# Top-k attention and an ELU layer on one core: scores at the head of a step, the last keys' chunk turned with the first half, values a step later

## Chip, cores and metric

One core of one Trainium2 chip runs the whole program as one launch. The metric is device time in microseconds (us); lower is better. The engines are called PE (TensorE matmuls; PEld are its weight loads), DVE (VectorE), ACT (ScalarE), POOL (GpSimd) and SP (SyncE, here a queue of DMA issues).

## What is computed

Eight batches of eight heads, 576 rows, head size 64. Of each row of scores only the 32 largest count; then a softmax, and the product with the values. The heads side by side are the rows of a layer with 2048 hidden columns and ELU between its two products.

```python
scores = scale * np.matmul(q, k.transpose(0, 1, 3, 2))
kth = np.partition(scores, -32, axis=-1)[..., -32:-31]
scores = np.where(scores >= kth, scores, -1e9)
attn = softmax(scores)                 # with 1e-9 added to the sum
x = np.matmul(attn, v)                 # (B,H,S,D) -> (B*S, H*D) = 4608 x 512
h = x @ w_in                           # 512 -> 2048
out = np.where(h > 0, h, np.exp(np.minimum(h, 0)) - 1) @ w_out   # 2048 -> 512
```

## The kernel before

**Steps.** A batch's 576 queries are four tiles of 128 (`qt` 0 to 3) and one of 64 (`qt` 4); a step is one such tile with a pair of heads (of the small tile, four heads). There are 144 steps. Each passes through four stages in successive steps of one loop (L809): in step n the scores of step n + 2 are computed (`ahead`), DVE selects the 32 largest of step n (`cur`), ACT and POOL mask and normalise step n - 1 (`prev`), and PE turns the weights of step n - 2 (`done`).

**Stages.** `scores` (L326) runs four matmuls, two per head, into two wide PSUM tiles (`wide[0]`, `wide[1]`, one per head, printed as scps), which ACT copies to SBUF (L343). `select` is a generator with four passes of DVE's MAX8 and MATCH_REPLACE8 (L355 to L369). `spread` (L376) takes the gap between threshold and maximum on POOL, `mask` (L396, L397) makes the exponentials on ACT, once per head, and `normalise` (L407 to L414) divides on POOL. `turn` (L418) transposes the weights on PE and copies them on ACT (L434) into a tile `et`: four chunks of keys of the first head (`main`), the chunk that holds the last 64 keys of both heads (`rest`), and four chunks of the second head (`other`). `main` and `other` use two PSUM tiles in turn (eps); `rest` uses free columns of `wide[1]`, the tile of the second head's scores. When the last step of a group (one tile or a pair) has been turned, the group is appended to `closing`, and `attend` (L443) multiplies it with the values (avps) and copies the result to `xT` (L486).

**The layer.** When a block's `xT` is complete (a block has one or two slots of 128 rows; the first five and the last have one, fifteen have two), `ffn_pieces` appends its work to a list: sixteen `hidden` pieces (four accumulated matmuls each, L534), whose results ACT reads in groups (L544 to L553), and then the second product: for one slot four `project` pieces (L562), for two slots seven `product` pieces (L624) of a scheme with seven block products, for which POOL combines the operands (L580) and SP streams kept differences of weights (`tw`, L666). A piece has a nominal cost in us: hidden 1.1 or 1.85, project and product 3.55.

**The order.** Every engine executes its instructions in the order in which the loop writes them. `feed` is called four times a step (the quarters q1 to q4) and takes as many pieces as a plan allows: each block has a due time in steps (`ready`, L728) and the cost of all blocks ahead of it (L729 to L733), and the rate is the smallest of what is left to each due time, so that the pieces last until the next block is ready (L772). So PE gets, in step n: q1, scores, attention, q2, main, q3, rest, other, q4. ACT's copies and masks stand between in the same order. `load_v` and `load_halves` are put on SP at fixed steps ahead of a batch; a value tile is one of five buffers and is loaded again when its last `attend` is done.

Of the kernel before, what the change touches and what calls it, by code (L numbers as in the profile page):

```python
# [80 lines left out]
def kernel(  # L81
# [119 lines left out]
    def hook():  # L201

        if decode:
            decode.pop(0)()
# [121 lines left out]
    def scores(u):  # L326

        u.sc = scpool.tile([P, 2, S], FP32, tag="sc", name="sc")
        q0 = (QUERIES if u.t.b == 0 else S) + u.t.qt * P
        for half in range(2):  # L330
            for h, i, rows in u.heads:
                kq = kqT[u.t.b, h // 2]
                part = slice(i * D, (i + 1) * D)
                k0 = (KEYS if i == 0 and u.t.b == 0 else 0) + half * HS
                nc.tensor.matmul(  # L335
                    wide[i][rows, half, 0:HS],
                    kq[part, q0 : q0 + u.t.ql],
                    kq[part, k0 : k0 + HS],
                    start=True,
                    stop=True,  # L340
                )
        for i in range(2):
            nc.scalar.activation(  # L343
                u.sc[:, i, :].rearrange("p (a s) -> p a s", a=2),
                wide[i][:, :, 0:HS], AF.Copy, scale=scale,
            )

    def select(u, more=False):

        u.first = small.tile([P, 2, 8], FP32, tag="m1", name="m1")  # L350
        u.last = small.tile([P, 2, 8], FP32, tag="m4", name="m4")
        cur = [u.sc[:, i, :] for i in range(2)]
        found = [u.first[:, i, :] for i in range(2)]
        for i in range(2):
            nc.vector.max(found[i], cur[i])  # L355
        if more:
            hook()
        yield
        wk = [wkpool.tile([P, S], FP32, tag=f"wk{i}", name="wk")[:] for i in range(2)]
        for r in range(TOP_K // 8 - 1):  # L360
            for i in range(2):
                nc.vector.match_replace(wk[i], found[i], cur[i], TAKEN)  # L362
            cur = wk
            for i in range(2):
                if r < TOP_K // 8 - 2:
                    found[i] = small.tile([P, 8], FP32, tag=f"m{i}", name="m")[:]
                else:
                    found[i] = u.last[:, i, :]
                nc.vector.max(found[i], cur[i])  # L369
            hook()  # L370
            yield
# [46 lines left out]
    def turn(u, chunks):  # L418

        if u.turned:  # L420
            return
        g = u.group
        if g.et is None:
            g.et = etpool.tile([P, 2 * J + 1, len(g.tiles), P], FP32, tag="et", name="et")
        if chunks.stop - chunks.start == 1:
            ps = wide[1][:, 1, HS : HS + P]
        else:
            ps = ps_t.tile([P, JP], FP32, tag="t", name="eps")
        sc = u.sc[:, :, :].rearrange("p i s -> p (i s)")
        n = chunks.stop - chunks.start  # L430
        for c in range(n):
            c0 = (chunks.start + c) * P
            nc.tensor.transpose(ps[:, c * P : (c + 1) * P], sc[:, c0 : c0 + P], ident[:])  # L433
        nc.scalar.copy(  # L434
            g.et[:, chunks, u.at, :],
            ps[:, 0 : n * P].rearrange("p (c q) -> p c q", c=n),
        )
        if chunks.stop == 2 * J + 1:
            u.turned = True
            if u.at == len(g.tiles) - 1:  # L440
                closing.append(g)

    def attend(g):  # L443
        t = g.tiles[0]
        ps = ps_t.tile([P, JP], FP32, tag="t", name="avps")
        n = P if t.rem else sum(x.ql for x in g.tiles)
        for k in range(2 if t.rem else 1):
            hp = 2 * g.hp + k if t.rem else g.hp
            vt = vT[t.b, hp]
            for c in range(J + 1):  # L450
                for i in range(2):
                    chunk = J if c == J else i * (J + 1) + c
                    w = g.et[:, chunk, :, :].rearrange("p a q -> p (a q)")
                    cols = slice(0, n)
                    if t.rem:
                        c0 = R * (k if i == 0 else 1 - k)
                        w = w[:, c0 : c0 + R]
                        cols = slice(k * R, (k + 1) * R)
                    nc.tensor.matmul(  # L459
                        ps[i * D : (i + 1) * D, cols],  # L460
                        vt[:, 2 * J + i if c == J else i * J + c, :],
                        w,
                        start=(c == 0),
                        stop=(c == J),
                    )
        if t.rem:
            finish(t.block, 2, slice(2 * g.hp, 2 * g.hp + 2), t.cols,
                   ps[:, 0:n].rearrange("p (a q) -> p a q", a=2))
            return
        c0 = 0  # L470
        tiles = list(g.tiles)
        while tiles:
            blk, lo, parts = tiles[0].block, tiles[0].cols.start, 0
            while tiles and tiles[0].block is blk:
                parts += 1
                hi = tiles.pop(0).cols.stop
            finish(blk, parts, g.hp, slice(lo, hi), ps[:, c0 : c0 + hi - lo])
            c0 += hi - lo

    def finish(blk, parts, at, cols, src):  # L480
        if blk.xT is None:
            if blk.slots == 1:
                blk.xT = xpool.tile([P, NC, P], FP32, tag="xT", name="xT")
            else:
                blk.xT = late["x"].tile([P, NC, T], FP32, tag="xT", name="xT")
        nc.scalar.copy(blk.xT[:, at, cols], src)  # L486
        blk.left -= parts
        if blk.left == 0:
            ffn.extend(ffn_pieces(blk))

    gates = []
    place = [0]
# [195 lines left out]
    blocks, tight = [], 2 * NHP  # L688
# [10 lines left out]
    while ends:  # L699
        n = 1 if len(blocks) <= J else 2  # L700
# [5 lines left out]
    for b in range(B):  # L706
        first[b] = len(steps)
        tiles = []
        for qt in range(J + 1):
            r0 = b * S + (JP if qt == J else qt if b == 0 else qt * P)  # L710
            if qt == J:
                (blk, slot), c0, n = slots[b | 1, J], (b % 2) * R, R
                rows = slice(r0, r0 + R)
            else:
                (blk, slot), c0, n = slots[b, qt], 0, P
                rows = slice(r0, r0 + J * (P - 1) + 1, J) if b == 0 else slice(r0, r0 + P)
            c0 += slot * P
            t = Tile(b, qt, rows, blk, slice(c0, c0 + n))
            blk.left += NHP
            blk.tiles[slot].append(t)  # L720
            tiles.append(t)
        for qts in orders[b]:
            for hp in range(NHP // 2 if qts == (J,) else NHP):
                group = Group([tiles[qt] for qt in qts], hp)
                steps += [Step(tiles[qt], hp, group, i) for i, qt in enumerate(qts)]
            for qt in qts:
                n = len(steps)
                tiles[qt].block.ready = n + 2.0 if n <= tight else n + 2.5  # L728
    NS = len(steps)  # L729
    total = 0.0  # L730
    for blk in sorted(blocks, key=lambda x: x.ready):
# [72 lines left out]
    def step(n):  # L804
        return steps[n] if 0 <= n < NS else None

    closing = []
    main, rest, other = slice(0, J), slice(J, J + 1), slice(J + 1, 2 * J + 1)
    for n in range(NS + 3):  # L809
        for fn, args in todo.pop(n, []):  # L810
            fn(*args)
        ahead, cur, prev, done = step(n + 2), step(n), step(n - 1), step(n - 2)
        passes = select(cur, n < tight) if cur else iter(range(4))
        if prev and n > tight:
            spread(prev)
        next(passes)
        feed(n, 0.25)
        if ahead and n > 1:
            scores(ahead)
        while closing:  # L820
            attend(closing.pop(0))
        if prev:
            mask(prev, 0, n <= tight)
        if n > 1:
            turn_qk()
        next(passes)
        feed(n, 0.25)
        if done:
            turn(done, main)
        if prev:  # L830
            mask(prev, 1, n <= tight)
        next(passes)
        feed(n, 0.25)
        if done:
            turn(done, rest)
            turn(done, other)
        next(passes)
        if prev:
            normalise(prev)
        if spare and n >= first[1] - 2:  # L840
            difference(*spare.pop(0))
        feed(n, 0.25)
        turn_qk(True)
        if n < 2:
            scores(ahead)
# [36 lines left out]
```

## Time and profile before

| | |
|---|---|
| three runs | 1586.64, 1590.04, 1593.43 us; median 1590.04 |
| the profiled execution | 1590.94 us, its span 1588.4 us |
| mean granted TensorE clock | 0.988 of full speed |
| DMA | 123.47 MB, 78 GB/s |
| MAX8 over 576 columns, one | 748 ns |
| exponential with its sum over 576 columns, one | 776 ns, and 187 ns to read the sum |
| copy of 128 x 512 turned weights, one | 581 ns |
| scaling of 128 x 576 weights on POOL, one | 755 ns |

The profile comes from one execution. In its rows, "x4" is a count, and in rows in order of time the first two numbers are the start and the length in us of a run of like instructions; "[1.25 <-ACT et L434]" says that the engine was idle 1.25 us ahead of it, until ACT's operation of line 434 on the tile et was done. A matmul that the program writes once appears as two records (and two weight loads), the transposes as one.

### The profile page before, as it was taken

How to read it: one execution, taken by the hardware profiler on the slowest of the kernel's cores; microseconds unless marked ns; L12 is line 12 of the kernel's file. 1: busy time of each engine (PE TensorE's matmuls, PEld its weight loads, DVE VectorE, ACT ScalarE, POOL GpSimd, SP SyncE). 2: the span in 40 equal slices, each digit the busy share in tenths (PEclk: the TensorE clock that was granted, in tenths of full speed). 3: DMA queues.
4: the chain of work that ended last, by engine and by line, in shares of the span. 5: the costliest groups of instructions: out<-in, count | busy, mean ns of one | idle time of the engine just before them, and what ended most of it. 6: DMA issues, size and time to landing. Idle time of an engine off the chain costs nothing.

```text
span 1588.4 us, 28211 instructions
## 1 busy us (share of the span) xinstructions
PE 1516.6 (95%) x9492; PEld 1182.4 (74%) x9492; DVE 1451.2 (91%) x2976; ACT 1200.0 (76%) x2460; POOL 904.0 (57%) x1551
## 2 busy tenths in 40 slices
PE   4679999999999999999999999999999999999999
PEld 2467767767778778877887778777787777877786
DVE  6899999999999899999999699999999969999700
ACT  6897777878786868686968687868777777878652
POOL 4983455556555565646565656565655565656550
PEclk9889999999999999999999999999999999999999
DMA  8522201233405140424122323224130513030311
GB/s 242 192 80 37 38 30 56 56 70 79 120 1 150 31 135 17 132 33 127 39 91 60 97 61 88 71 65 108 50 94 27 138 42 116 19 110 1 119 54 34
DMA packets 224911, 123.47 MB, mean 78 GB/s; under 512 B 182272, under 2 KB 183296, under 8 KB 224768
## 3 DMA queue, kind: packets, MB, share of 16 engines
q1 hardware_dynamic: 223568, 121.38, 28.2%
q8 instruction: 75, 1.23, 0.3%
q14 instruction: 68, 0.56, 0.1%
q10 hardware_dynamic: 1200, 0.30, 0.1%
HBM read 108.00 MB, written 13.63 MB: 77 GB/s over the span
## 4 chain that ended last, share of the span: by engine, by line
PE 72%; ACT 12%; DVE 9%; POOL 3%; issue 3%; SPq 1%; DMA 1%; DVEq 0%; ACTq 0%; POOLq 0%
PE hps L534 24%; PE ops L624 20%; PE avps L459 10%; PE scps L335 9%; PE eps L433 6%; DVE wk L362 4%; DVE m L369 3%; PE ops L562 3%; ACT sc L397 2%; ACT sc L396 2%; ACT sc L343 2%; DVE m L355 1%; ACT et L434 1%; ACT n L553 1%; ACT n L544 1%
## 5 line engine op out<-in xcount | busy, mean ns | idle before, releaser
L369 DVE MAX8 m<-wk 128x8 f32<-128x576 f32 x864 | 610.1, 748 | 2.2 <-POOL den L376 2.2
L534 PE MATMUL hps<-xT,w_in 128*128 128x256 f32 (+1 forms) x2688 | 548.6, 353 | 0.4 <-ACT gT L547 0.4
L534 PEld LDWEIGHTS hps<-xT,w_in 128*128 128x128 f32 x2688 | 440.6, 192 | 59.7 <-issue 18.8
L362 DVE MATCH_REPLACE8 wk<-m,wk 128x576 f32<-128x576 f32 x576 | 423.7, 744 | 0.0
L407 POOL TENSOR_SCALAR dene<-den 128x2 f32<-128x2 f32 x144 | 32.8, 228 | 466.0 <-ACT sc L397 464.6
L397 ACT ACTIVATE sc<-sc,den 128x576 f32<-128x576 f32 x288 | 223.4, 776 | 55.6 <-POOL den L376 40.8
L335 PE MATMUL scps<-kqT 64*128 64x288 f32 (+1 forms) x1280 | 215.0, 445 | 52.4 <-ACT et L434 38.4
L343 ACT ACTIVATE sc<-scps 128x576 f32<-128x576 f32 x288 | 170.7, 644 | 82.9 <-PE scps L335 82.9
L396 ACT ACTIVATE sc<-sc,m 128x576 f32<-128x576 f32 x288 | 223.8, 777 | 4.8 <-DVE m L369 4.8
L624 PE MATMUL ops<-tw,gT 128*128 128x256 f32 x960 | 220.0, 382 | 2.7 <-POOL gT L580 1.3
L414 POOL TENSOR_SCALAR sc<-sc,rec 128x576 f32<-128x576 f32 x288 | 214.2, 755 | 14.9
L355 DVE MAX8 m<-sc 128x8 f32<-128x576 f32 x288 | 202.1, 744 | 11.9 <-ACT sc L343 11.9
L362 DVE MATCH_REPLACE8 wk<-m,sc 128x576 f32<-128x576 f32 x288 | 211.8, 744 | 0.0
L335 PEld LDWEIGHTS scps<-kqT 64*128 64x128 f32 (+1 forms) x1280 | 113.6, 182 | 131.4 <-ACT et L434 53.5
L624 PEld LDWEIGHTS ops<-tw,gT 128*128 128x128 f32 x960 | 177.7, 190 | 33.4 <-issue 7.3
L504 POOL TENSOR_TENSOR gT<-n,gT 128x512 f32<-128x512 f32 x136 | 173.7, 1279 | 28.9 <-ACT n L553 27.7
L459 PE MATMUL avps<-et,vT 128*64 128x256 f32 (+2 forms) x2320 | 187.5, 312 | 0.0
L459 PEld LDWEIGHTS avps<-et,vT 128*64 128x64 f32 x2320 | 127.8, 142 | 68.0 <-issue 28.5
L433 PE MATMUL eps<-ident,sc 128*128 128x128 f32 x1152 | 175.2, 277 | 0.0
L434 ACT COPY et<-eps 128x512 f32<-128x512 f32 x288 | 167.4, 581 | 9.8 <-PE eps L433 8.2
L624 PE MATMUL ops<-w_out,gT 128*128 128x256 f32 x720 | 164.2, 381 | 0.0
L433 PEld LDWEIGHTS eps<-ident,sc 128*128 128x128 f32 x1152 | 138.3, 143 | 30.8 <-issue 12.9
(56 smaller groups left out, 1536.7 us busy)
## 6 DMA issues: line engine op xcount, KB each, us to landing
tw<-kept SPq DMA_DIRECT2D x240, 256.0 KB, 3.0
raw<-in_moe_w_in_dram SPq DMA_DIRECT2D x16, 512.0 KB, 4.9
vT<-in_v_dram SPq DMA_DIRECT2D x64, 128.0 KB, 2.5
raw<-in_moe_w_out_dram SPq DMA_DIRECT2D x16, 512.0 KB, 4.0
out_dram<-osb SPq DMA_DIRECT2D x32, 256.0 KB, 3.7
kin<-in_k_dram SPq DMA_DIRECT2D x112, 72.0 KB, 2.7
qin<-in_q_dram SPq DMA_DIRECT2D x112, 72.0 KB, 2.6
kept<-tw SPq DMA_DIRECT2D x16, 256.0 KB, 2.1
```

What stands on the lines that cost most here:

```text
L335: nc.tensor.matmul(wide[i][rows, half, 0:HS], kq[part, q0 : q0 + u.t.ql], kq[part, k0 : k0 + HS], start=True, stop=True,)
L343: nc.scalar.activation(u.sc[:, i, :].rearrange("p (a s) -> p a s", a=2), wide[i][:, :, 0:HS], AF.Copy, scale=scale,)
L355: nc.vector.max(found[i], cur[i])
L362: nc.vector.match_replace(wk[i], found[i], cur[i], TAKEN)
L369: nc.vector.max(found[i], cur[i])
L396: nc.scalar.activation(sc, sc, AF.Prelu, scale=-1.0, bias=low, alpha=1.0 / STEEP)
L397: nc.scalar.activation(sc, sc, AF.Exp, scale=-STEEP, bias=gap, accum_out=u.den[:, i : i + 1])
L414: nc.gpsimd.tensor_scalar(u.sc[:, i, :], u.sc[:, i, :], rec[:, i : i + 1], 1.0, ALU.mult, ALU.mult)
L433: nc.tensor.transpose(ps[:, c * P : (c + 1) * P], sc[:, c0 : c0 + P], ident[:])
L459: nc.tensor.matmul(ps[i * D : (i + 1) * D, cols], vt[:, 2 * J + i if c == J else i * J + c, :], w, start=(c == 0), stop=(c == J),)
L534: nc.tensor.matmul(blk.h[:, f % bank, :], w_in[:, i, f * P : (f + 1) * P], blk.xT[:, i, 0:n_tok], start=(i == 0), stop=(i == NC - 1),)
L624: nc.tensor.matmul(sums, x[:, f, :], w, start=opens and f == 0, stop=f == NG - 1, skip_group_check=not opens,)
```

## The change

The scores of step n + 2 move to the head of step n, ahead of the first quarter's pieces (and ahead of `spread`). From step 12 on (`settled`) until the last step, a closed group is attended at the head of a step, right behind the scores, and only if it was closed more than one step ago; `closing` therefore holds the step in which the group was closed. Before step 12 and after the last selection the attention stays behind q1. `turn(done, rest)` moves from the third quarter to the second, right behind `turn(done, main)` and ahead of the second mask. The due times of all blocks that are ready after step 8 grow from n + 2.5 to n + 3.25.

So PE's order in a step becomes: scores, attention, q1, q2, main, rest, q3, other, q4.

```diff
         if chunks.stop == 2 * J + 1:
             u.turned = True
             if u.at == len(g.tiles) - 1:
-                closing.append(g)
+                closing.append((place[0] // 4, g))
...
-                tiles[qt].block.ready = n + 2.0 if n <= tight else n + 2.5
+                tiles[qt].block.ready = n + 2.0 if n <= tight else n + 3.25
...
-    closing = []
+    closing, settled = [], tight + 4
...
         passes = select(cur, n < tight) if cur else iter(range(4))
+        if ahead and n > 1:
+            scores(ahead)
+        steady = settled <= n < NS
+        while steady and closing and closing[0][0] < n - 1:
+            attend(closing.pop(0)[1])
         if prev and n > tight:
             spread(prev)
         next(passes)
         feed(n, 0.25)
-        if ahead and n > 1:
-            scores(ahead)
-        while closing:
-            attend(closing.pop(0))
+        while closing and not steady:
+            attend(closing.pop(0)[1])
         if prev:
             mask(prev, 0, n <= tight)
...
         if done:
             turn(done, main)
+            turn(done, rest)
         if prev:
             mask(prev, 1, n <= tight)
         next(passes)
         feed(n, 0.25)
         if done:
-            turn(done, rest)
             turn(done, other)
```

## The prediction

> **What bounds the kernel now.** I read the page first: busy shares, then the span in 40 slices.
>
> ```profile
> span 1588.4 us, 28211 instructions
> PE 1516.6 (95%) x9492; PEld 1182.4 (74%) x9492; DVE 1451.2 (91%) x2976; ACT 1200.0 (76%) x2460; POOL 904.0 (57%) x1551
> PE   4679999999999999999999999999999999999999
> DVE  6899999999999899999999699999999969999700
> ```
>
> PE and DVE are both full after the third slice. Which of them leads shows in the waits of the whole span, longest in total first (who <- whom: us, times, longest):
>
> ```profile
> ACT sc L343 <- PE scps L335: 82.9, 88, 4.0
> DVE gT L506 <- ACT n L549: 70.7, 4, 62.1
> DVE kqT L289 <- PE scps L335: 33.0, 3, 16.1
> ```
>
> DVE waits for PE, three times up to 16 us, and ends its selection 62 us before its last additions. PE is the late engine, so the time is PE's work plus PE's lost time, and the change leaves the work as it is: the same matmuls, in another order. The question is what PE loses today. Two stretches answer: from 115 us, when the FFN has begun to fill PE, to 455, and from there to the end (columns: us, busy of PE, PEld, DVE, ACT, POOL, clock, DMA).
>
> ```profile
> 115.00:455.00 340.00, 332.60 (x2206) 243.70 (x2204) 340.00 (x700) 261.02 (x534) 180.59 (x341) 0.99 0.23 57
> 455.00:1588.00 1133.00, 1115.17 (x6906) 887.82 (x6906) 1012.54 (x2084) 844.94 (x1739) 637.77 (x1085) 1.00 0.28 74
> ```
>
> PE idles 7.4 us in the first and 17.8 us in the second. The waits of PE (first two rows, 455 to the end) and of its weight loads (third row, same stretch; fourth row, 115 to 455) name the cause:
>
> ```profile
> PE scps L335 <- ACT et L434: 10.9, 12, 1.3
> PE scps L433 <- ACT sc L343: 2.3, 3, 0.8
> PEld scps L335 <- ACT et L434: 19.4, 17, 1.8
> PEld scps L335 <- ACT et L434: 9.0, 8, 2.4
> ```
>
> The scores wait for a copy of turned weights. The matmul row understates it, because a matmul record runs on after PE could have taken the next; the load row (19.4 us) is nearer. One such event, in order of time (ACT's and PE's rows):
>
> ```profile
> 450.84 0.56 ACT L434 COPY et<-eps 128x512 f32<-128x512 f32 x1
> 450.96 0.27 PE L433 MATMUL scps<-ident,sc 128*128 128x128 f32 x1
> 451.07 0.60 PE L433 MATMUL eps<-ident,sc 128*128 128x128 f32 x4
> 451.30 0.77 ACT L396 ACTIVATE sc<-sc,m 128x576 f32<-128x576 f32 x1
> 451.50 1.89 PE L534 MATMUL hps<-xT,w_in 128*128 128x256 f32 x8
> 452.88 0.58 ACT L544 ACTIVATE n<-hps 128x512 f32<-128x512 f32 x1
> 453.33 0.75 PE L335 MATMUL scps<-kqT 64*128 64x288 f32 x2
> 455.03 0.25 ACT L434 COPY et<-scps 128x128 f32<-128x128 f32 x1
> 455.33 1.24 PE L335 MATMUL scps<-kqT 64*128 64x288 f32 x6 [1.25 <-ACT et L434]
> 456.50 2.38 PE L459 MATMUL avps<-et,vT 128*64 128x256 f32 x20
> ```
>
> The last keys' chunk (`rest`, L835) is turned by PE at 450.96 into the bank of the second head's scores. Its copy stands on ACT behind the second mask (451.30 to 452.88, 1.6 us) and a pair of hidden pieces (452.88 to 455.03, 2.15 us). The scores begin at 453.33, stop after the first head's half, and end at 456.50: 3.17 us. Undisturbed they take 1.17:
>
> ```profile
> 445.79 1.24 PE L335 MATMUL scps<-kqT 64*128 64x288 f32 x8
> 446.96 1.99 PE L534 MATMUL hps<-xT,w_in 128*128 128x256 f32 x8
> ```
>
> So this event costs 2.0 us where the matmul row shows 1.25.
>
> **The change, part by part.** The sum is made against the profiled execution, 1590.9 us (span 1588.4, 2.5 around it); it lies 0.9 over the median of 1590.04.
>
> *Rest turned with main.* Removes nothing; the one transpose and the copy (0.14 us to the next operation on ACT) move ahead of the second mask and the third quarter's pieces. In the event above the copy would have started at 451.30 instead of 455.03, 3.7 us earlier and 2 us before the scores want the bank. Where a finished pair of hidden pieces now stands ahead of the main copy (q2 in the built order of the changed kernel), it comes 2.15 us later, at 453.5, and still ends 0.4 us too late; I count some eight of the fifteen two-slot blocks with such a step ahead of the scores, and three with scores right after the turning. I leave 11 x 0.5 = 5 us standing of the 19.4 after 455: **-14 us** (bounds: 0, if ACT's backlog only moves; -24, if all go and each costs 0.3 us more than its load row, as 2.0 against at most 1.8 above suggests).
>
> *Scores at the head of the step.* They pass the first quarter's pieces. Order on PE was q4, q1, scores, attention; it is q4, scores, attention, q1. The distance from `rest` to the scores was other, q4, q1; it becomes q3, other, q4: the same on average. The three waits of `rest` for the scores' copies (2.3 us) come where nothing lies between; the built order has two such steps left: **-1 us**. The first mask on ACT now stands behind the copies of q1 too; that is the slower rival.
>
> *Values held over a step.* `attend` runs one step later. What waits behind it: the xT copy, so FFN input, answered by the due times (3.25 for 2.5). SP's v loads now wait for attention in their own step instead of the one before:
>
> ```profile
> SPq L269 <- PE avps L459: 85.4, 8, 44.0
> tw<-kept SPq DMA_DIRECT2D x240, 256.0 KB, 3.0
> ```
>
> Behind a v load on SP stand `tw` loads released by products of the same step, which follow that attention on PE: 0 us (if one were held a step, PE would wait up to 10 us, at most at the eight blocked places).
>
> *Due times 0.75 step later.* L725 to L733 and `feed` pace the pieces evenly: 975.8 us of pieces before the last block over 146.5 - 6 steps are 6.95 us a step, so the plan stands 0.75 x 6.95 = 5.2 us behind. On a PE that is always full that costs nothing. But PE is not free to run ahead in the first stretch: its main transposes need POOL's normalisation, which needs DVE's selection of the step before.
>
> ```profile
> 204.73 1.48 POOL L414 TENSOR_SCALAR sc<-sc,rec 128x576 f32<-128x576 f32 x2
> 206.23 0.60 PE L433 MATMUL eps<-ident,sc 128*128 128x128 f32 x4
> 393.34 1.48 POOL L414 TENSOR_SCALAR sc<-sc,rec 128x576 f32<-128x576 f32 x2
> 398.74 0.66 PE L433 MATMUL eps<-ident,sc 128*128 128x128 f32 x4
> ```
>
> At 206 us PE starts 0.02 us after the normalisation ends, at 399 us 3.9 us after. Until about 455 us DVE therefore sets the pace, and what PE saves there (9.0 us of waits) or puts off turns into idling, except for that 0 to 4 us of room, say 4 (bounds 0 and 8, as the normalisation itself comes earlier when PE does): **-4 us**. The work put off comes back behind it: 5.2 us, and one attention of 2.4 us (row at 456.50) that is open half of the time, 1.2: **+6.5 us**.
>
> *Clock.* After one such wait, at 701 us, the granted clock falls (the number behind the five busy times), and once more in the stretch from 1000 us:
>
> ```profile
> 650.00:700.00 50.00, 50.00 (x300) 40.55 (x300) 50.00 (x105) 39.19 (x79) 26.71 (x49) 1.00 0.39 96
> 700.00:750.00 50.00, 47.97 (x267) 36.16 (x266) 50.00 (x103) 34.22 (x73) 31.23 (x52) 0.97 0.39 93
> 1000.00:1050.00 50.00, 48.74 (x264) 37.63 (x264) 50.00 (x105) 41.74 (x85) 24.60 (x48) 0.97 0.14 29
> 703.84 3.94 PE L459 MATMUL avps<-et,vT 128*64 128x256 f32 x20
> ```
>
> The same twenty matmuls take 3.94 us there against 2.38, so 1.6 us are lost. Without those waits I take **-2 us** of 3.2 (bounds 0 and -3.2). The Trainium skill, "TensorE: Matmul & The Clock Gate", Part 1, says otherwise: the array is throttled only after an idle window of about 3.4 us. By that rule waits of 1.3 us are not the cause, and the 2 us would not come back; the trace shows the drop right behind such a wait, in a stretch where PE idles 2.0 us in all.
>
> *New small waits* from the tighter pairing of two products around the main and rest transposes: 0 to 4, I take **+2 us**.
>
> Sum: -14 - 1 - 4 + 6.5 - 2 + 2 = **-12.5, about -12 us**: 1579 profiled, 1578 beside the median.
>
> **The rivals.**
> *The backlog stays (no change).* ACT is full wherever four hidden pieces stand in a step, so the wait only changes its place, and DVE's pace eats the rest. For it: the row 452.88, pieces ahead of a copy. Half of the 14 and no room: -7 - 1 + 6.5 - 1 + 2 = 0, with the room -4: 1586 to 1590.
>
> *The mask comes late (slower).* In product steps ACT now copies q1's product before the first mask. Today:
>
> ```profile
> 713.98 3.62 PE L624 MATMUL ops<-w_out,gT 128*128 128x256 f32 x16
> 713.87 0.19 ACT L397 ACTIVATION_READ_ACCUMULATOR sc<-sc,den 128x1 f32 x1
> 716.10 1.49 POOL L414 TENSOR_SCALAR sc<-sc,rec 128x576 f32<-128x576 f32 x2
> 718.70 0.66 PE L433 MATMUL eps<-ident,sc 128*128 128x128 f32 x4
> 720.29 2.37 POOL L580 TENSOR_TENSOR gT<-gT 128x1024 f32<-128x1024 f32 x1
> ```
>
> From the last mask to the end of normalisation are 3.7 us (713.87 to 717.59), and PE starts 1.1 us later. With the product first, both masks end 0.4 (copy) + 3.3 (two masks) + 0.6 (copies) = 4.3 us after the product, the normalisation at 8.0; PE's next main transposes come 0.5 + 3.6 + 0.5 + 1.2 + 3.6 = 9.4 us after it. The 1.4 us left hold until a 2.37 us combination stands ahead of the normalisation on POOL: then PE waits 1 us. Over some thirty product steps without attention that is 30 us against the 12 gained: 1609; at half of them 1594. ACT keeps its order in the event above, where the small copy of 455.03 passes nothing. The Trainium skill, the same page, "Architectural detail: the array is 16× 32×32, not 1× 128×128", calls ACT's queue a strict FIFO; by it the mask cannot pass the product's copy, and the trace agrees.
>
> *More is gained.* All of the 24 us and 8 us of room: about -26, 1564.
>
> **How the numbers follow.** Forecast (-7 to -20) 0.55; more gained 0.07; no change 0.22; slower 0.16. A measurement of this kernel can tell about 0.5%, 8 us, from no change: faster needs under 1582.1, slower over 1598. Most of the forecast's case and the greater gain lie below: faster 0.57; same 0.28; slower 0.15. The range from 1565 to 1597 leaves out the far ends of the last two.
>
> **What would show it.** Right: the rows "scps L335 <- ACT et L434" fall to a third after 455 us, PE's idle time there falls to under 10 us while it grows between 115 and 455, DVE's waits on kqT shrink, and no clock drop follows 701 us. Wrong: a new PE wait for POOL L414 at the transposes (mask late), or PE waiting for `et` as before. The forecast fails too if PE's busy time itself grows: the new order would then drain PE more often between matmul shapes.

## The result and the profile after

Eight runs of each kernel: before 1590.96 us (1586.64 to 1593.43), after **1582.94 us** (1582.14 to 1585.47). The ratio is 0.995, with a 95% interval from 0.9939 to 0.9961: 8 us faster, 0.5%. The forecast was 1578 us, 12 us faster, with a range from 1565 to 1597. The profiled execution of after took 1585.47 us, the longest of its eight; its span is 5.1 us shorter than that of before, so some 2.5 of the 8 us stand in no trace.

The page of after, the lines that answer to those of before:

```profile
span 1583.3 us, 28148 instructions
PE 1522.8 (96%) x9492; PEld 1189.1 (75%) x9492; DVE 1450.6 (92%) x2976; ACT 1189.6 (75%) x2460; POOL 901.2 (57%) x1551
```

The waits of the whole span:

```profile
DVE gT L506 <- ACT n L549: 76.3, 4, 67.7
ACT sc L343 <- PE scps L335: 37.3, 51, 2.4
DVE kqT L289 <- PE scps L335: 24.7, 2, 16.6
```

DVE still ends its selection 68 us before its last additions, and still waits for PE, in two places where there were three. PE stays the late engine. ACT waits for scores less often (51 times for 88; the scores now come a quarter earlier in the step); that saves nothing by itself.

The windows of after (us, busy of PE, PEld, DVE, ACT, POOL, clock, DMA):

```profile
0.00:115.00 115.00, 76.92 (x382) 55.10 (x382) 98.13 (x194) 94.70 (x191) 84.58 (x125) 0.86 0.59 178
115.00:455.00 340.00, 331.38 (x2189) 241.39 (x2189) 340.00 (x700) 256.57 (x528) 180.07 (x343) 0.98 0.24 58
455.00:1583.00 1128.00, 1114.48 (x6925) 892.57 (x6923) 1012.46 (x2084) 838.29 (x1742) 636.50 (x1085) 1.00 0.28 74
```

PE's idle time is 8.6 us in the second stretch (7.4 before) and 13.5 in the third (17.8 before). PE's busy time grew by 6.2 us over the span, but not in the work of the third stretch: before had 1516.6 - 332.6 - 1115.2 = 68.8 us in the first 115 us, after has 76.9, at a granted clock of 0.86. DVE sets the pace there, so that costs nothing. The clock drop behind the wait at 701 us is gone (1.00 between 700 and 750 us, 0.97 before), and so is the one after 1000 us; a new one stands at 1136 us (the last section shows it). Between 200 and 455 us after has more of them: the clock is 0.93 from 200 to 250 us and from 350 to 400, where before has one stretch of 0.97 (250 to 300).

The waits of PE and of its weight loads (first four rows from 455 us on, the last from 115 to 455):

```profile
PE scps L335 <- ACT et L434: 5.8, 7, 1.1
PE eps L433 <- POOL sc L414: 1.2, 1, 1.2
PE scps L433 <- ACT sc L343: 1.1, 2, 0.7
PEld scps L335 <- ACT et L434: 10.6, 12, 1.5
PEld scps L335 <- ACT et L434: 9.2, 6, 3.9
```

The scores still wait for `et`: 10.6 us by the load row, 19.4 before. The step that leaves DVE's pace can be seen directly. First before, then after: DVE's first MAX8 of one and the same step, and PE's main transposes in it.

```profile
454.46 1.40 DVE L355 MAX8 m<-sc 128x8 f32<-128x576 f32 x2
460.64 0.60 PE L433 MATMUL eps<-ident,sc 128*128 128x128 f32 x4
```

```profile
454.69 1.40 DVE L355 MAX8 m<-sc 128x8 f32<-128x576 f32 x2
456.71 0.60 PE L433 MATMUL eps<-ident,sc 128*128 128x128 f32 x4
```

PE stood 6.2 us behind DVE's start and now stands 2.0 behind it. It reaches this point 3.9 us earlier, of the 5.1 us by which the span shrank; so all the rest of the run, some 1127 us, brought 1 us, though the waits fell by 9 us there and one of two clock drops went. The windows from this same point to the end, first before, then after, show where it went:

```profile
460.64:1588.40 1127.76, 1109.87 (x6873) 884.22 (x6871) 1006.90 (x2072) 841.38 (x1732) 634.89 (x1081) 1.00 0.28 74
456.71:1583.30 1126.59, 1112.77 (x6917) 891.12 (x6915) 1010.75 (x2081) 836.83 (x1740) 635.23 (x1083) 1.00 0.28 74
```

From the same step on, after has 44 matmul records more to do. They are three hidden pieces (eight records each, 1.89 us by the row at 451.50 in the prediction) and one attention (twenty records, 2.38 us): an estimated 8.0 us. This work that was put off came back and took up nearly all that the shorter waits gave. The lost time itself fell by about 9 us (8.0 + 1.2). Forecast for it were 15 us (-14 - 1 - 2 + 2); what holds the other 6 us is the question for the experiments.

The waits that are left are of two kinds (ACT's and PE's rows of after, in order of time). Four of PE's seven are like this one:

```profile
1112.84 0.75 PE L335 MATMUL scps<-kqT 64*128 64x288 f32 x2
1113.18 0.63 ACT L553 ACTIVATE n<-n 128x512 f32<-128x512 f32 x1
1113.72 0.57 ACT L434 COPY et<-eps 128x512 f32<-128x512 f32 x1
1114.18 0.27 ACT L434 COPY et<-scps 128x128 f32<-128x128 f32 x1
1114.51 1.23 PE L335 MATMUL scps<-kqT 64*128 64x288 f32 x6 [0.92 <-ACT et L434]
```

A finished pair of hidden pieces, whose last operation is L553, stands on ACT ahead of the main copy, and the copy of `rest` behind that. Three are like this one:

```profile
1049.64 0.27 PE L433 MATMUL scps<-ident,sc 128*128 128x128 f32 x1
1050.25 0.78 ACT L397 ACTIVATE sc<-sc,den 128x576 f32<-128x576 f32 x1 [2.65 <-POOL den L376]
1050.28 0.75 PE L335 MATMUL scps<-kqT 64*128 64x288 f32 x2
1051.02 0.35 ACT L632 COPY e<-ops 128x256 f32<-128x256 f32 x1
1051.28 0.58 ACT L434 COPY et<-eps 128x512 f32<-128x512 f32 x1
1051.75 0.28 ACT L434 COPY et<-scps 128x128 f32<-128x128 f32 x1
1052.08 1.23 PE L335 MATMUL scps<-kqT 64*128 64x288 f32 x6 [1.05 <-ACT et L434]
```

No piece stands in q3 or q4 here, so the scores of the next loop turn, now at its head, come 0.64 us after the transpose of `rest`. ACT is not behind with work: its first mask waits 2.65 us for POOL's `spread`, and the product's copy and both copies of turned weights are queued behind it.

### The profile page after: what moved, and what is told of

Same layout as the page of the kernel before. It is cut to its first block, busy times and chain, and to the rows that moved or that the text cites. A ratio compares the mean times of both kernels' runs of the same rounds, so it can differ in the third digit from the quotient of the medians.

```text
span 1583.3 us, 28148 instructions
## 1 busy us (share of the span) xinstructions
PE 1522.8 (96%) x9492; PEld 1189.1 (75%) x9492; DVE 1450.6 (92%) x2976; ACT 1189.6 (75%) x2460; POOL 901.2 (57%) x1551
## 3 DMA queue, kind: packets, MB, share of 16 engines
q8 instruction: 75, 1.23, 0.3%
## 4 chain that ended last, share of the span: by engine, by line
PE 71%; DVE 17%; ACT 5%; issue 3%; POOL 3%; DMA 0%; SPq 0%; DVEq 0%; POOLq 0%; ACTq 0%
PE hps L534 25%; PE ops L624 23%; PE avps L459 9%; PE scps L335 9%; DVE wk L362 8%; DVE m L369 6%; PE eps L433 5%; DVE m L355 2%; ACT sc L397 1%; POOL sc L414 1%; DVE raw L192 1%; PE scps L433 1%; ACT et L434 1%; POOL gT L504 1%; ACT sc L396 0%
## 5 line engine op out<-in xcount | busy, mean ns | idle before, releaser
L335 PE MATMUL scps<-kqT 64*128 64x288 f32 (+1 forms) x1280 | 211.5, 447 | 37.4 <-ACT et L434 23.3
L414 POOL TENSOR_SCALAR sc<-sc,rec 128x576 f32<-128x576 f32 x288 | 213.5, 751 | 14.9
L343 ACT ACTIVATE sc<-scps 128x576 f32<-128x576 f32 x288 | 170.8, 646 | 37.4 <-PE scps L335 37.3
L459 PE MATMUL avps<-et,vT 128*64 128x256 f32 (+2 forms) x2320 | 191.9, 314 | 2.9 <-ACT et L434 2.9
L433 PE MATMUL eps<-ident,sc 128*128 128x128 f32 x1152 | 175.7, 277 | 2.1 <-POOL sc L414 1.6
L433 PEld LDWEIGHTS eps<-ident,sc 128*128 128x128 f32 x1152 | 143.4, 143 | 34.2 <-issue 7.0
L434 ACT COPY et<-eps 128x512 f32<-128x512 f32 x288 | 163.9, 569 | 6.3 <-PE eps L433 5.8
```

The lines of the kernel that those rows point to most:

```text
L335: nc.tensor.matmul(wide[i][rows, half, 0:HS], kq[part, q0 : q0 + u.t.ql], kq[part, k0 : k0 + HS], start=True, stop=True,)
L414: nc.gpsimd.tensor_scalar(u.sc[:, i, :], u.sc[:, i, :], rec[:, i : i + 1], 1.0, ALU.mult, ALU.mult)
L459: nc.tensor.matmul(ps[i * D : (i + 1) * D, cols], vt[:, 2 * J + i if c == J else i * J + c, :], w, start=(c == 0), stop=(c == J),)
```

## The experiments

All ten kernels compute the whole reference. Their times stand beside before's on the same chip: 1591.49 us for e1 to e4, 1590.71 for e5 to e8, 1590.65 for e9 and e10. The theory at the start was the prediction's: `rest` turned early earns the gain, the due times give part of it back. The rival: the gain is eaten by new waits of the moved scores and attention.

### One part alone: rest early (e1)

```diff
             turn(done, main)
+            turn(done, rest)
...
-            turn(done, rest)
             turn(done, other)
```

> The kernel before with one part of the change: the last keys' chunk is turned right behind the main chunks; scores, attention and due times as before. Theory (the early turning is what gains, the late due times and the held attention give part of it back): the copy of the chunk then has q3, other, q4 and q1 ahead of the scores, so the weight loads of the scores wait under 3 us for et after 455 us (19.4 before, 10.6 with the whole change), no work is put off, and the time is 1573 +- 5 us, below the whole change. Rival (ACT's backlog only moves, and the place of the scores is what gains): 1585 to 1591, with more than 10 us of such waits left.

Measured 1579.60 us, ratio 0.9926 [0.9914, 0.9939]: 12 us faster, and 1.6 us above the end of the expected range. No load of the scores waits for `et` after 455 us any more. What took its place (waits of PE after 455 us, then one event in order of time, in which the scores were computed just ahead of the first row):

```profile
PE scps L433 <- ACT sc L343: 9.1, 12, 0.8
PE avps L459 <- ACT et L434: 3.1, 7, 0.5
```

```profile
1039.20 0.66 PE L433 MATMUL eps<-ident,sc 128*128 128x128 f32 x4
1039.30 1.19 ACT L343 ACTIVATE sc<-scps 128x576 f32<-128x576 f32 x2 [0.79 <-PE scps L335]
1040.64 0.30 PE L433 MATMUL scps<-ident,sc 128*128 128x128 f32 x1 [0.78 <-ACT sc L343]
```

`rest` goes into the bank that the scores have just filled. Moved forward, it meets them: it waits until ACT has copied both heads. The same bank makes the wait at either end, and moving one user only changes which neighbour it touches. No run gave `rest` a bank of its own. The theory's direction held; the expected size left out this second wait and the smaller one of the attention for the copies (the second row).

### One part alone: scores at the head (e2)

```diff
+        if ahead and n > 1:
+            scores(ahead)
         if prev and n > tight:
             spread(prev)
         next(passes)
         feed(n, 0.25)
-        if ahead and n > 1:
-            scores(ahead)
```

> The kernel before with the scores alone at the head of the step; the chunk turned late, the attention behind q1, due times as before. Theory: from the chunk's turning to the scores only other and q4 are left, so the waits of the scores for et grow to 40 us or more after 455 us, and PE changes matmul shape twice more a step (scores, pieces, attention): slower, 1605 to 1625 us. Rival (the place of the scores gains by itself): at or below 1585.

Measured 1678.29 us, ratio 1.0545 [1.0531, 1.056]: 87 us slower, the direction as expected, the size over twice that. Loads of PE from 115 us on, first before, then e2, and DVE's waits in e2:

```profile
PEld scps L335 <- ACT et L434: 28.4, 25, 2.4
```

```profile
PEld scps L335 <- ACT et L434: 75.1, 51, 3.8
DVE m L355 <- ACT sc L343: 62.6, 22, 11.9
```

With `rest` late and the scores early, only `other` and q4 lie between the transpose and the scores. The load row grows by 46.7 us in 26 more waits. The mean granted clock falls from 0.988 to 0.971; what the clock takes is (1 - 0.971) x 1676.6 = 48.6 us of full speed against 19.1 in before, 29.5 more. The two make 76 of the 87 us, and DVE now starves for scores, so PE's lateness counts in the first stretch too. This account is from the rows; no run took the clock away by itself.

### One part alone: the due times (e3)

```diff
-                tiles[qt].block.ready = n + 2.0 if n <= tight else n + 2.5
+                tiles[qt].block.ready = n + 2.0 if n <= tight else n + 3.25
```

> The kernel before with the due times of n + 3.25 alone. Theory (the start up to 455 us is paced by DVE, so work put off comes back at the end): 3 to 5 us slower, 1594 to 1596, PE's idle time between 115 and 455 us up by 2 to 5 us from 7.4. Rival (PE is full all along, so when a piece runs does not matter): within 1 us of before.

Measured **1572.51 us**, ratio 0.9881 [0.9868, 0.9895]: 19 us faster. The theory fell here. It took a later due time as work put off, a few us of loss; alone it is the largest gain of the three, and larger than the whole change. The window from the step compared above (the main transposes at 456.45 us here) to the end, and the waits from 455 us on:

```profile
456.45:1570.30 1113.85, 1107.32 (x6897) 885.40 (x6895) 1010.17 (x2079) 842.37 (x1736) 633.72 (x1083) 1.00 0.27 75
```

```profile
PE scps L335 <- ACT et L434: 1.1, 5, 0.3
PEld scps L335 <- ACT et L434: 6.0, 11, 0.8
```

PE idles 6.5 us where it idled 17.9, though `rest` is turned as late as in before. The stretch is 13.9 us shorter than before's although 24 records more, three hidden pieces, lie in it. In the step that was the prediction's example:

```profile
450.15 0.75 PE L335 MATMUL scps<-kqT 64*128 64x288 f32 x2
450.31 0.63 ACT L553 ACTIVATE n<-n 128x512 f32<-128x512 f32 x1
450.84 0.25 ACT L434 COPY et<-scps 128x128 f32<-128x128 f32 x1
451.14 1.23 PE L335 MATMUL scps<-kqT 64*128 64x288 f32 x6 [0.25 <-ACT et L434]
```

The hidden pieces have moved to other quarters, the copy of `rest` behind the pair starts 0.69 us after PE begins the scores (450.84 against 450.15) instead of 1.70 us after (455.03 against 453.33), and the wait is 0.25 us for 1.25. A due time does not only say how far behind the plan runs: it decides in which quarter of which step each piece falls, and that pattern repeats from block to block.

The new theory: what costs is the number of steps in which a finished pair of hidden pieces (2.15 us on ACT) stands just ahead of the copy of `rest` while the scores follow closely on PE, and any shift of the plan changes that number. The rival: a later due time is better in itself, since PE then always has pieces in store. They part on due times on either side, and in the new order.

### Other due times, both orders (e4 to e7)

Each changes the one constant of the line above: after's order with 2.5 (e4) and 3.5 (e7), before's order with 2.75 (e5) and 3.5 (e6).

```diff
-                tiles[qt].block.ready = n + 2.0 if n <= tight else n + 2.5
+                tiles[qt].block.ready = n + 2.0 if n <= tight else n + 2.75
```

> The changed kernel with the due times of before (n + 2.5), though its attention comes a step later. Theory (work put off costs): 3 to 5 us faster than the changed kernel, 1578 to 1580, unless the pieces run out ahead of a block's attention. Rival (the late due times are needed, as the blocks are complete 0.75 step later): PE idles ahead of the late blocks, 1585 or more, with steps without pieces.

> The kernel before with due times of n + 2.75 alone. Theory now (a due time sets in which quarters the pieces fall, and so how many steps have the scores too close behind the last keys' chunk; the built order has 18 such steps after step 30 with n + 2.5, 3 with n + 3.25 and 1 with 2.75): 1570 to 1575 us, under 8 us of waits of the scores' weight loads for et after 455 us. Rival (late due times gain by themselves, the later the better): a third of the way from 1591 to 1572, about 1585.

> The kernel before with due times of n + 3.5 alone. Theory (the quarters decide): 12 such steps, eight among hidden pieces at 2 us and four among products at 0.85 us, 19 us against 6 us for n + 3.25: 1583 to 1588, slower than with 3.25. Rival (the later the better): at or below 1572.

> The changed kernel with due times of n + 3.5. Theory (the quarters decide): none of its steps has the scores too close behind the chunk, so the 10.6 us of waits after 455 us go: 1567 to 1572. Rival (work put off is paid at the end): a quarter step more, 1.7 us slower than the change, 1584 to 1586.

| due time | before's order | after's order |
|---|---|---|
| n + 2.5 | 1590.96 (before) | 1571.08, ratio 0.9872 [0.9858, 0.9885] (e4) |
| n + 2.75 | **1567.19**, 0.9853 [0.9834, 0.9871] (e5) | not run |
| n + 3.25 | 1572.51, 0.9881 [0.9868, 0.9895] (e3) | 1582.94, 0.995 [0.9939, 0.9961] (after) |
| n + 3.5 | 1577.95, 0.9919 [0.9901, 0.9938] (e6) | 1569.46, 0.9865 [0.9846, 0.9884] (e7) |

Loads of PE from 455 us on, for e5, e6 and e7:

```profile
PEld scps L335 <- ACT et L434: 2.6, 4, 0.7
```

```profile
PEld scps L335 <- ACT et L434: 6.5, 10, 1.8
```

```profile
PEld scps L335 <- ACT et L434: 1.4, 3, 0.5
```

Later is not better: in before's order the time falls from 1591 to 1567 and rises again to 1578. The new order is 20 us faster than the old at 2.5, 10 slower at 3.25 and 8 faster at 3.5. So the rival falls. The expected directions came in all four; the sizes missed in three: e4 came out 7 us below its range, e5 3 and e6 5.

For the theory speaks a count in the traces, of the steps after 455 us in which ACT's operation directly ahead of the copy of `rest` is the end of a hidden pair (L553) and the scores start less than 3.2 us behind the transpose. Before has 10 such steps, e6 7, e3 3 and e5 none. But such a step costs only where the copy comes late: PE stops for 1.25 to 1.30 us in seven of before's ten and for 1.29 us in one of e6's; in all others, e3's three too, for 0.22 us at most. Seven stops at the 2.0 us of the prediction's example, and the two clock drops of 1.6 us behind two of them, are an estimated 17 us. That is most of the 19.6 us that e3 saves from the same step on (13.9 us, and 5.7 for the three pieces). After has no such step, as its `rest` is copied right behind `main`; its twelve waits are of the two kinds shown above, and at 3.5 there are three.

The number of such steps does not carry everything: e6 loses to e3 by 5.4 us with nearly the same load row (6.5 and 6.0 us). Work put off has its price as well. From the same step on, e5 and then e6:

```profile
458.24:1564.40 1106.16, 1097.61 (x6873) 879.52 (x6871) 1009.83 (x2078) 839.69 (x1732) 631.99 (x1081) 1.00 0.29 76
458.15:1573.60 1115.45, 1108.61 (x6905) 888.12 (x6903) 1008.84 (x2077) 846.58 (x1740) 636.01 (x1083) 1.00 0.28 75
```

e5 has as many records left as before, e3 three pieces more, e6 four. At 1.89 us a piece that is 5.7 of the 7.7 us by which e3's stretch is longer than e5's, and 1.9 us where e6's is 1.6 longer than e3's; e6 also comes to this step 1.7 us later than e3. (e6's profiled execution was the fastest of its five; the remaining 2 us to its median stand in no trace.) So the first theory's price for work put off was real, and in e3 a larger gain hid it.

In e4 the list of pieces runs dry in the last quarters of some steps (in 29 of the 289 stretches between the transposes its pieces differ from before's). That does no harm: the scores wait there for `et` in three loads only, 1.0 us in all after 455 us.

e5 beats both kernels, before by 24 us and after by 16, with one constant changed. It has still one lost place, a DMA wait of PE ahead of a product:

```profile
906.10 3.46 PE L624 MATMUL ops<-tw,gT 128*128 128x256 f32 x8 [3.42 <-DMA tw<-kept]
```

### The parts together at one due time (e8 to e10)

At 3.25 the same pieces lie between the same transposes in the traces of e3, e8, after, e9 and e10 (in all 289 stretches), so that only the order of the parts differs. e8 is before with the due times and the early `rest`. e9 is after with `rest` back in the third quarter. e10 is after without the hold:

```diff
-        while steady and closing and closing[0][0] < n - 1:
+        while steady and closing and closing[0][0] < n:
```

> Due times of n + 3.25 and the chunk turned early; scores and attention where the kernel before has them. The pieces fall into the same quarters as in the changed kernel and as with the due times alone. Theory: no scores wait for et, but the chunk now follows the scores with little between wherever q2 is empty (the product steps), and waits 0.8 us there for ACT's copy of the scores, some twenty times without attention: 1580 to 1590, slower than the due times alone (1572.5). Rival (the early chunk gains in any plan, as it did with n + 2.5): 1560 to 1570.

> The changed kernel with the last keys' chunk turned in the third quarter again, as before the change; the pieces fall into the same quarters as in the changed kernel. Theory: between the chunk and the next scores only other and q4 are left, and q4 is empty in 49 steps after step 30, 37 of them product steps: 37 x 0.85 and 12 x 2 us, 55 us of waits against 15 us in the changed kernel, so 1615 to 1630 us. Rival (with the attention next to the scores the late chunk does little; the 87 us of the scores alone were the shape changes): 1583 to 1595.

> The changed kernel, but a closed group is attended at the head of the very next step instead of one step later; the pieces fall into the same quarters. Theory: the values now need ACT's copy of the last four chunks, which stands behind the second mask and q3's pieces, with only q4 and the scores between: PE waits at avps for et in some fifty steps, 0.3 to 1 us each, 1590 to 1620 us. Rival (the copy is there in time, the holding over is worth nothing): within 3 us of the changed kernel, 1580 to 1586.

| at n + 3.25 | us | ratio to before |
|---|---|---|
| due times alone (e3) | 1572.51 | 0.9881 [0.9868, 0.9895] |
| and rest early (e8) | 1581.24 | 0.9938 [0.9922, 0.9955] |
| and scores at the head, values held (after) | 1582.94 | 0.995 [0.9939, 0.9961] |
| after, rest late (e9) | 1687.24 | 1.0601 [1.0583, 1.0619] |
| after, values not held (e10) | 1615.75 | 1.0166 [1.0143, 1.0189] |

Waits after 455 us in e8, from 115 us on in e9 (the second row is DVE's, of the whole span), and after 455 us in e10:

```profile
PE scps L433 <- ACT sc L343: 10.5, 17, 0.8
```

```profile
PEld scps L335 <- ACT et L434: 89.6, 56, 4.0
DVE m L355 <- ACT sc L343: 65.0, 31, 12.0
```

```profile
PEld avps L459 <- ACT et L434: 26.7, 22, 2.9
```

e8 hit: where few waits for `et` are left, turning `rest` early only buys the wait for the scores' copy, 17 times, and 8.7 us of time. e9's direction held and its size was again over twice the expected; e10's time hit, by fewer and longer waits than the fifty of 0.3 to 1 us that were expected. Without the hold, values meet weights that were turned just ahead of them and whose copies are not done. The three moves need each other: scores at the head lose 104 us without the early `rest` and 33 without the hold. Together they are no gain at this plan, as they cost 10.4 us against e3. From the same step on that shows as 13.8 us of idling instead of 6.5 and 5.4 us more of busy time; of these 5.4, the attention held over is 2.4 and the clock drop at 1136 us 1.7.

## Why the prediction was right, and where it was not

The sign and the range held; the size, 12 us, came out as 8. The sum did not come about as it was put together, and that it lay so near is in part luck. Of the signs of being right, the smaller wait of DVE for kqT, PE's growing idle time before 455 us and the end of the drop at 701 us came. The waits for `et` fell to a little over half instead of a third, and PE's idle time after 455 us to 13.5 us instead of under 10.

- **What bounds the kernel**: held. PE led in every run, and what counted was its lost time, above all the scores' wait for the copy of `rest`.
- **Rest turned with main, -14**: too large. The waits fell by 8.8 us, not by 14. I left 5 us standing, 0.5 for each of eleven steps of just the two kinds shown above, and 10.6 stand. The kinds were right and the price was not: in the examples the scores take 2.90 and 3.03 us from the start of the first row to the end of the last (1114.51 + 1.23 - 1112.84, and 1052.08 + 1.23 - 1050.28) instead of 1.24, so 1.7 and 1.8 us each. And the prediction took this price as that of the move; e1 (-12) and e8 against e3 (+8.7) show that it depends on the plan, down to the sign.
- **Scores at the head, -1**: "the same on average" for the distance from `rest` holds only with the early `rest`; by itself this move costs 87 us (e2). The -1 itself came: the three waits of `rest` for the scores' copies (2.3 us) became two (1.1 us).
- **Values held, 0**: within the change no new wait of any size shows. The hold is what the new place of the attention needs (e10: +33 without it).
- **Due times 0.75 later, -4 and +6.5**: the step that failed, though its sizes nearly held. The room of 4 us in the first stretch was there (3.9 by the two rows at 456 and 460 us). What was put off is 8.0 us by the 44 records: 5.7 for the pieces, where 5.2 were reckoned, and 2.4 for an attention that is open whole, not half. What failed is what the step left out: it moved all pieces back by 5.2 us and kept their pattern. But the quarters change with it. In before's order the later due time brings 19 us (e3), in after's it costs 11.9 (e4 against after). So the 12 us that I forecast came near for another reason: a new order worth 20 us at 2.5, less a phase of the plan that suits it badly.
- **Clock, -2**: after 455 us the drops behind the wait at 701 us and after 1000 became one drop at 1136; about the half of 3.2 us. Over the whole span the mean granted clock fell, from 0.988 to 0.984; the new drops lie where DVE sets the pace.
- **New small waits, +2**: one new row of a named wait, 1.2 us (POOL L414, the next point). The row L433 <- L343 of 1.1 us is not new, and belongs to the -1.
- **The mask late on ACT**: one wait of 1.2 us for POOL L414. The rival did not come as priced; but a first mask that waits does hold the copies behind it, in the three steps like that at 1050 us. **The backlog stays**: partly so; 10.6 of 19.4 us, in fewer and other steps.

What is open: of what after loses to e3 from the same step on, 12.7 us in the profiled executions, 7.3 are idle time and 4.1 the attention and the clock drop; the last 1.3 us stand in the busy time and were not taken apart. That the late copies cause the loss is read from the traces and from shifting the plan; no run took the finished pairs off ACT with all else the same. In e2 and e9 the clock and DVE's starving were not separated by a run.

## What to carry to other kernels

Where a planner deals pieces into slots, a constant of the plan is also a phase: before judging a reordering, run it and the old order over a few values of that constant, for a difference at one value (here +10, -8 or -20 us) says little about the order. When two uses share a bank, look at the wait at both ends: moving one away from its late neighbour moves it toward the other. And a move that looks neutral "on average" has to be counted in the steps where nothing lies between.

## What the runs showed of the hardware

The granted clock fell behind short waits. In after:

```profile
1135.41 1.23 PE L335 MATMUL scps<-kqT 64*128 64x288 f32 x6 [1.06 <-ACT et L434]
1136.58 4.06 PE L459 MATMUL avps<-et,vT 128*64 128x256 f32 x20
```

Twenty such matmuls take 4.06 us behind a visible wait of 1.06 us. Behind the wait of 1.05 us at 1052.08, also in after, they take 2.38, so that wait cost no clock:

```profile
1053.24 2.38 PE L459 MATMUL avps<-et,vT 128*64 128x256 f32 x20
```

The Trainium skill, "TensorE: Matmul & The Clock Gate", Part 1, puts the throttle behind an idle window of about 3.4 us. e5's DMA wait of 3.42 us, behind which eight product matmuls took 3.46 us (1.89 in the run of eight ahead of it), agrees with that; the drop at 1136 us does not, by the idle time that the rows show. What else in the microseconds ahead of it counted as idle, no run here tells.

PE's idle time understates what waits cost: in e1 it is 17.0 us from the compared step on, hardly less than before's 17.9, and yet this stretch is 8.1 us shorter, with the same 6873 records. It is the busy time that fell, from 1109.9 to 1102.6 us:

```profile
458.27:1577.90 1119.63, 1102.62 (x6873) 877.33 (x6871) 1007.84 (x2073) 841.77 (x1732) 634.60 (x1081) 1.00 0.28 75
```

Some 3.2 of these 7.3 us are before's two clock drops. Much of the rest is likely time lost in waits that stands in the busy time of the waiting matmuls' records, as in the prediction's example, which costs 2.0 us where its row shows 1.25. So two kernels are compared better by the length of a stretch, begun at the same step, than by its idle time.
